# Values of a sliding-window attention kernel: staged per head with a ones column, moved 256 tokens at a time, read contiguously

## The chip, the cores and the metric

The kernel runs on one core of a Trainium2 chip. The core has a matrix engine (PE, whose weight loads are shown as a row of their own, PEld), three engines that work elementwise (DVE, ACT, POOL) and a sequencer, SP, that issues the DMA transfers; each of them takes its instructions in order and waits on semaphores. The metric is the device time of one execution in microseconds, as the median of the runs shown. Shorter is better.

## The reference

Two layers are run one after the other with the same weights; each is an attention block and a token mixer, both on normalised rows and both added to x. x has 2048 tokens of 512 values, 32 heads of 16 values, and a window of 256 tokens.

```python
def _A_ref(x, wqkv, wo):
    B, S, D = x.shape
    H = 32; Dh = D // H; W = 256
    qkv = (x @ wqkv).reshape(B, S, 3, H, Dh).transpose(2, 0, 3, 1, 4)
    q, k, v = qkv[0], qkv[1], qkv[2]
    scores = jnp.einsum("bhqd,bhkd->bhqk", q, k) * (Dh ** -0.5)
    idx = jnp.arange(S)
    mask = (idx[:, None] - idx[None, :] >= 0) & (idx[:, None] - idx[None, :] < W)
    scores = jnp.where(mask[None, None], scores, -1e9)
    p = softmax(scores, axis=-1)
    o = jnp.einsum("bhqk,bhkd->bhqd", p, v)
    return o.transpose(0, 2, 1, 3).reshape(B, S, D) @ wo

def _B_ref(x, w1, b1, w2, b2):
    h = layernorm(x)
    u = gelu(einsum("bsd,sf->bdf", h, w1) + b1)
    y = einsum("bdf,fs->bds", u, w2) + b2
    return y.transpose(0, 2, 1)

for _ in range(2):
    x = x + _A_ref(layernorm(x), A_wqkv, A_wo)
    x = x + _B_ref(layernorm(x), B_w1, B_b1, B_w2, B_b2)
```

## The kernel before

The program is a graph of operations. Each is created once, with the engine or engines that may run it, what it reads and what it writes. `ORDER`, a packed constant, holds the sequence of all 2487 operations and the engine chosen for each; `begin_order` unpacks it, `replay` hands out buffers in that sequence, and `emit` writes one instruction stream per engine and puts a wait wherever a result comes from another engine. So the order of the work is written out by hand beforehand, and nothing is decided on the chip. `cost`, `issue` and `prio` are figures for the search that made `ORDER`; in the program as it stands they do nothing.

**Attention.** Tokens are taken in four groups of 512 (`qkv`, m = 0 to 3). Normalised rows are transposed to xhT, on PE for the first group and by a DMA on SP (`tr`, L538) for the rest. PE makes keys (`fk`), queries (`fq`) and values (`fv`), all at L509 in steps of two 512-column matmuls (four of 256 columns in the split first group). DVE or ACT copies each result out of PSUM: L567 for queries, L589 for keys (staged in stg) and L619 or L621 for values (`evv`). The keys go on to kbd either by DVE or POOL (L603) or by eight small transfers on SP (`kz`, L598).

**Values.** `vproj` runs once for 128 tokens. Its copy goes to vst, ordered by half, by value index e and by group r of heads. Then `vz` (L624) issues four transfers on SP, one for each half of the tokens and each half h of the heads; each brings 64 partitions of 512 bytes to vb. In vb, [P, 3, 8, 17, 16], a block of 64 tokens has 17 rows of 16: 16 value indices and a row of ones, with the 16 heads of a half next to each other. The ones are written once per slot at the start, as three memsets on POOL (L457), and make the matmul produce the softmax denominators as a 17th output row. vb holds three groups of tokens, vst four blocks of 128 tokens.

**Scores and outputs.** For a chunk of queries, `sc` (L677) writes scores of 32 rows per head into two pairs of PSUM banks, four heads side by side on PE. ACT exponentiates each pair (`exp`, L692), POOL masks the blocks at the edge of the window (L713), and `pv` (L730) multiplies: eight matmuls of 64 rows by 17 columns side by side on PE, for two halves h and four heads r. The weights of each are 17 values of vb, `vb[64h:64h+64, slot, jj, :, 4o+r]`, so they lie 16 elements (32 bytes) apart. DVE transposes the result (L750), takes reciprocals (L754), POOL or DVE multiplies (`prod`, L756), and DVE transposes back (L761). `fwo` is the output projection, added to x at L772. Each of the two layers has 76 score groups, 152 exponentials of up to 1024 columns and 32 `pv` operations, which stand in the order mostly two by two.

**Mixer.** `fu` and `ful` (L509, L851) make u from w1 tiles that stream in (L786), ACT applies gelu (L866), and `fy` (L509) multiplies with w2 tiles (L798) and is added to x at L892. `fu`, `fwo`, `fy` and the projections are the fillers that `ORDER` puts between the score groups on PE. In the second layer the attention begins while the first layer's `fy` is still running.

The steps that the prediction follows are these: on SP the transfers `vz`, `kz`, `tr`, `w1` and `w2`; on DVE and ACT `evv`, `evk`, `evq` and `evka` (L577, L578); on POOL masks and `prod`; on PE `fv`, `sc` and `pv`. What replaces `vproj` and its two call sites is printed with the change; the old forms are here.

Of the kernel before, what the change touches and what calls it, by code (L numbers as in the profile page):

```python
# [15 lines left out]
    'c-qBRKd9<h8b8r<-^-mj1Bc}dWZ(?sK^8KQffOk+kbw-O$PN}Rq)6dHiY&NbVUdLt7VctU;erbm7P45lV38t)g@uI+78Vv378Vv37Pqjtg~csyv0uDiu'  # L16
    'ipFK%qy0iFL-l2f4}ed{l4GvqAn7}dL4-^Y&W9FK~WT%(O<(5BZQA1+h*2}9%D>xHJJLH3%1|yT{8@V?M~kOBzc~`vh^Qlvl(NfWV=f=N!1jhPNo~_8%'
    'a_WssH#W4F*zwwSw1dxtzru2BcA%jM7$n7`9rW)QIbm_I>t*j^q1Phnw8sl4O8ww`i*wimJ#TWJS^>#&!y2V?|N0i2G3#C4{P~s(c6M)M~YQJw%7$9T;'
    '0I7MsmxYgv}gIak)}8RyI8d{LcqKAjZ`+MaD6k)x`sc4xMq&24);ws*T-r_*Y+)*EngE`2kdPG<8Nv}Le#l`hi-;~rmg#wJrP!oEL7IR3g?jXF_P*I{M'
    '3R*uVY6vc5rj^j>;MbYEqV-!ctW|IY?h#QSYGf?WaI*DRJNU>N9!>|;FUZui<I<<eIw9KpAr*7fl;lZ_B*Ky{F<(F(q!9D19A6%ExKvjq8zHiy4F))l?'  # L20
    'j}e2!O+7YrqojtqPO0nO-<On9NvZCYvK_jF*mhDZCJA+=%q+?3bUK<M=|i0lhrOQE1AN6^uZ_D1OT68tmGPJ{DOs=A1kOe~zTG}NR@?2b3EAD>HwuM<<'
    '2c(ph+u+l?>C#t;jnSnR(q+Ysb$%#(Q36C3<kqNX5;ZVjz@#Zw9Ht)pQMTVPqW{5nBC&MQmND${XV4)Qmc2AZkNXrIM)UY<9Y)gal75t8=~kq)y)3vl*'
    '<laCyGiLO!>XC-z$o4h-*#L78+5f)2Xdn#2jf_qCl`8+MRBv+bhAQCD9N4dOh}a&+}lh=S7jOGstj>r@jK6oEg3@X^tz2reZKd*VZ##*A1PB!;z|~Oi?'
    'JkB_iasRs$|7)oO(hP6+e7uZl%ll3W)EOt;jK!c~Sf9dm`t8q|_Rj#kq&jHwEbNQmgVWmjTU;)Wq{HlH45obpk&lBQ{QfMDIN*v@Rzxm&Itmm6EmjElE'
    '@ur%%uMaH17fx4w8VK7t^8RsJ5(Cj%78+a+2L}ZnMt|)B18jnO0h|Pw~RiFwHkr<SMO08B3N@2MKW+}ieFc}B7<NBTsm6U<7-5Lhcb*Z^&$_z`0HwR-`'
    'NqM5-y432?CT-Nq%_gNxqERFvqL)e#Zk9F6(h$n<Qe4eZ6csqNn-@3k9~7u)HAxah8Oej)_hV)Bq1j5)4{{IuHdPe<qtz7uR{utdGq@|d?l>R@K@fz_p'
    '7S7tO83j(`cN>71@w~1q?euNLV_x8xstN*$eL=Q!r0d=1~@&B>Dbp+grI`#07#0i#RWn%hB3Bm3&}F#$VAA{F@8!JQ51x@O!}*Yh=a)lc4;$63FuE_RF'
    '6}=T21s=hXRixkr?H_xFJZAX()!A?cZn|8u(%VcSV*t(@aoOe1k{wXgURIkHD((b~hMox24jbN;8Zn;7B@c|BjYXNcspt5#0<r$mr^NuiNWFMiUS=U2i'
    '7{p<WO59v^$X9>zEAn8wXGXV>k!cw&R!X$nHwfr_a3-8ddJNwwZ1W=tAkBdV8S3{?X!t|3${7NMjILD&fjrJ}!4k@<tDNuuZ$5RxPtc;FbiZkfxau~@)'
    '{hFj1ycZAa|+zo?&Lm--Frx*}1jN;v$VKj|sy*4c<@5;2oOw$VfmGJ;RiV1bZ4hN`JK&fVIM?i+*P}Pw9GthN5pKDsAX=53UlF@iHh6BEJLQxX^VFEN9'  # L30
    'cGbb4+e_0F0tD~?1CaW|0VH_f`+a}qL$&vNf$u|_TCJ+WTv>*+SAY`8p^{Vdio0F0SdCUI%52*%*p}_#qFyiz2$IJn0`A)mu`G}Cz3r&qscW>>VK=0x8'
    'l^BQ-rwIRnVHss8Zg4Js@3atl>?i>GI`NNO<nqEPN)akg~mUlgO*y!j)GVavRD#?W^>3ij?;8HMX(v<BN_~$(S=laB7!I|)`K=~mo&}LV%K*I1wbRPOC'
    '`Tp%$634nNC^;AYkf-W@ITf<!Y5d^~)U4gb;v%@^rx*N4F1$2SD&{kC3`kRk$QKD^*>tmec=CM~0!Qi-j7^menPMK)XQj0U5MfUDWZ!VkUVrp6QEO76-'
    ';3gK|J<2!df9L{q;LJ>T;!&nSrE4~C&-ddEg^;SZBNMyy3?=debP=oZ%B2&M_zfU+MNlp@0J_mD|cm3fj>I7Sm%gQOOV01(i<AI81@pxrK4kl~eM&kHN'
    'Qk5L6xLf=8YZxOd(VpK#$uYg<^a)Y`$a$G7_kzA%Uq$`)vIj4*jn9Javi#1-W6$(-T#J7%W8;{Y0&X9M%T;3S~!G>UMxz{o-1F69^Jm$+3J2PjBCrN_w'
    'of&P(IIAvk*rhcHV;%%$9j9@-I)Kyx8)V!uZTN{(z@^ftZTi0B)Evilp&A@KhAaZ-bl3ARh8wh2vu)kBR4oWFmQ@)ND@p8Vz+5CD;0yX}d;iPB?=G6hw'
    'txfyq0c<vT{ah1yz~gdMKk+?k2?yd5kbfwKgZGRl|OcW`RwfbJo*A(o{-Pyvk3CpM%R{uM>xLUK{JPrpU<<Kr@6VO13ocHKxd!NG2Pr8qk4*1xSD(XhL'
    '10N>1);$zPQ>sf6hz(V~1W%6~Mnsj5A;I!fEcwMd5_HaDx2Y5OTR3yy0)|V)GZ6PW`9%#je69pnN{(BLf0@b_Su>r1(XH4Cm4R%5rZSuV^U<*IqyS{Q~'
    'bbpwA10%ele}p)aZadi!%ug^#oAV@L|<x3aHZ==iz$$Q_yWTuLW4<-R<RU8d#BS1X?@O1PrWt9+c^_yXZ0Mn_s_yIvL67x*bHPixLqi1DlPyUib2cMSA'
    'QzWiG$$ltyp*K3W*ouYn@Hg`SY2u|*bj5+i?Q#|4K+<zf6XYCNqq!Qp7K<_g_&0@qaf`c)BqmB4w8~pC{PyBVwJq3GaasIVD!3)1;LjG;(q89*j=nXu%'  # L40
    'Yp$GC_ZW5VN`y`lB>YMp<gd!=T!zA%y1OX4m%)$D{JgTuowF!hXulx5IDL6nT+b2C!tx>?$4f-GoQ__4pZkR8UVNIF`}}hLv;e=tSP)(feR7@ft4IES?'
    'd7g}xvquZSVe!;{tIrGU@i'
# [263 lines left out]
def bass_interleave_layers__sliding_block__mixer_token_mlp__prompt_kernel(  # L306
# [28 lines left out]
    with es:  # L335
# [9 lines left out]
        vb = sb("vb", [P, 3, 8, 17, 16])  # L345
        vst = sb("vst", [P, NVS, 512])
# [30 lines left out]
        p_w1, p_ul, p_vs = Pool("w1", 4), Pool("ul", 2), Pool("vs", NVS)  # L377
# [153 lines left out]
        def qkv(m, before, split, layer):  # L531
# [81 lines left out]
            def vproj(sp):  # L613
# [9 lines left out]
                def f_vz(e):  # L623
                    return [e.dma_start(vb[64 * h:64 * h + 64, tk.slot, 2 * sp + i, 0:16],  # L624
                                        vst[64 * i:64 * i + 64, ts.slot, 256 * h:256 * h + 256].rearrange("p (e r) -> p e r", e=16)) for i in range(2) for h in range(2)]
# [346 lines left out]
```

## Time and profile before

| What | us |
|---|---|
| median of 3 runs | 446.96 (446.56 to 448.96) |
| the profiled execution | 448.0 |
| its span in the profile | 446.3 |
| PE busy | 415.7 (93%) |
| ACT busy | 317.6 (71%) |
| DVE busy | 311.5 (70%) |
| POOL busy | 230.0 (52%) |
| transfers vb<-vst | 128 of 32 KB, 1.9 to land (median) |

The profiled execution took 448.0 us, of which 446.3 lie inside the span that the profile covers and 1.7 around it; it was 1.0 us above the median. Busy time of PE counts an instruction from its start to its modelled end, so a busy PE is not PE at its peak. Engine names in the profile are followed by the line of the kernel and by the tiles written and read, such as "PS<-pt,vb". "SPq" is SP's queue of transfers. The column after the bar is busy time and mean duration of one; after the second bar stands the idle time in front of these instructions and what ended it. The TensorE clock that was granted is 1.00 throughout, so no time depends on it here.

### The profile page before, as it was taken

What the parts mean: (1) busy time and instruction counts of PE and PEld (TensorE: products, weight loads), DVE (VectorE), ACT (ScalarE), POOL (GpSimd) and SP (SyncE); (2) the same over time, 40 slices, a digit from 0 to 9 for tenths busy, and PEclk for the clock granted to TensorE, in tenths of its full rate; (3) what the DMA queues carried; (4) which work ended last, traced back from release to release, by engine and by line L of the source; (5) the groups of instructions that cost most, each with busy time, mean ns of one, the idle gap of its engine ahead of it and who ended that gap; (6) DMA issues with size and microseconds to landing.
All of it is one profiled execution on the core that took longest, in us unless ns stands there. A gap on an engine that the chain in (4) does not pass through costs nothing.

```text
span 446.3 us, 13926 instructions
## 1 busy us (share of the span) xinstructions
PE 415.7 (93%) x5923; PEld 192.3 (43%) x5992; DVE 311.5 (70%) x570; ACT 317.6 (71%) x361; POOL 230.0 (52%) x351
## 2 busy tenths in 40 slices
PE   7888788989989999999999999999999999999997
PEld 6544333333433444444434444443444444444444
DVE  6998799878796569466557869988885767520323
ACT  4998999989999932518888999999999861440000
POOL 3496968797687631010649658768786551000000
PEclk9999999999999999999999999999999999999999
DMA  8634321302323357221454161212223274744443
GB/s 246 186 73 128 74 50 32 85 10 34 93 56 84 109 160 217 84 61 49 127 111 109 44 172 37 61 36 57 59 52 75 67 208 123 201 128 144 118 143 106
DMA packets 99758, 44.71 MB, mean 100 GB/s; under 512 B 29936, under 2 KB 99696, under 8 KB 99696
## 3 DMA queue, kind: packets, MB, share of 16 engines
q1 hardware_dynamic: 99696, 43.82, 37.4%
q8 instruction: 47, 0.77, 0.7%
q14 instruction: 15, 0.12, 0.1%
HBM read 33.56 MB, written 2.10 MB: 80 GB/s over the span
## 4 chain that ended last, share of the span: by engine, by line
PE 69%; ACT 15%; DVE 5%; SPq 4%; DMA 3%; issue 2%; POOL 1%
PE PS L509 46%; ACT pt L692 15%; PE PS L851 8%; PE PS L677 7%; PE PS L730 7%; SPq L598 2%; DMA xhT<-xh_sb 2%; PE PS L392 1%; DVE stats L467 1%; DMA w2b<-in_B_w_dram 1%; SPq L624 1%; POOL pt L713 1%; DMA w1b<-in_B_w_dram 1%; DVE x_sb L772 0%; DVE ul L756 0%
## 5 line engine op out<-in xcount | busy, mean ns | idle before, releaser
L692 ACT ACTIVATE pt<-PS 128x1024 bf16<-128x1024 f32 (+1 forms) x304 | 281.9, 1032 | 20.1 <-PE PS L677 17.4
L713 POOL TENSOR_TENSOR pt<-pt,ldm 128x256 int32<-128x256 int32 (+2 forms) x270 | 177.6, 683 | 72.2 <-ACT pt L692 68.2
L509 PE MATMUL PS<-uT,w2b 128*128 128x512 bf16 (+1 forms) x287 | 68.1, 369 | 1.3 <-DMA w2b<-in_B_w_dram 0.8
L509 PE MATMUL PS<-xhT,wqkv 128*128 128x512 bf16 (+1 forms) x270 | 63.7, 355 | 5.8 <-ACT pt L692 2.1
L509 PE MATMUL PS<-xh_sb,w1b 128*128 128x512 bf16 x265 | 65.8, 380 | 3.4 <-issue 1.9
L677 PE MATMUL PS<-qT,kbd 32*128 32x256 bf16 (+4 forms) x1488 | 60.4, 251 | 4.7 <-ACT pt L692 1.4
L892 DVE SCALAR_TENSOR_TENSOR x_sb<-PS,b2col,x_sb 128x512 bf16<-128x512 f32 x31 | 22.8, 746 | 50.1 <-PE PS L509 49.9
L480 POOL TENSOR_TENSOR rstd<-agg,mhalf 128x2 f32<-128x2 f32 (+1 forms) x33 | 22.6, 689 | 58.2 <-DVE agg L469 58.1
L750 DVE STREAM_TRANSPOSE rl<-PS 128x1024 f32<-128x1024 f32 x32 | 39.8, 1245 | 16.6 <-PE PS L730 16.2
L730 PE MATMUL PS<-pt,vb 64*17 64x320 bf16 (+4 forms) x2976 | 45.0, 259 | 5.0 <-ACT pt L692 1.7
L677 PEld LDWEIGHTS PS<-qT,kbd 32*128 32x128 bf16 x1488 | 21.7, 92 | 63.1 <-ACT pt L692 40.1
L866 ACT ACTIVATE uT<-rl,b1col 128x512 bf16<-128x512 f32 x28 | 18.6, 713 | 39.6 <-DVE rl L862 39.5
L467 DVE BATCH_NORM_STATS2 stats<-x_sb 128x6 f32<-128x512 bf16 x64 | 42.8, 679 | 2.2 <-DMA x_sb<-in_A_x_dram 1.7
L730 PEld LDWEIGHTS PS<-pt,vb 64*17 64x17 bf16 x2976 | 35.0, 110 | 18.4 <-POOL pt L713 6.7
L509 PE MATMUL PS<-uT,pt 128*128 128x512 bf16 x163 | 41.1, 379 | 0.5 <-issue 0.3
L509 PEld LDWEIGHTS PS<-uT,w2b 128*128 128x128 bf16 x294 | 27.3, 98 | 31.9 <-issue 2.7
L851 PE MATMUL PS<-xh_sb,w1b 128*128 128x512 bf16 x164 | 37.8, 379 | 0.3 <-issue 0.2
L509 PEld LDWEIGHTS PS<-xh_sb,w1b 128*128 128x128 bf16 x280 | 23.9, 97 | 33.0 <-issue 6.1
L509 PEld LDWEIGHTS PS<-xhT,wqkv 128*128 128x128 bf16 x288 | 24.0, 97 | 31.7 <-issue 5.6
L509 PE MATMUL PS<-wqkv,xhT 128*128 128x512 bf16 x117 | 33.1, 381 | 3.5 <-issue 1.4
L509 PE MATMUL PS<-wo_sb,oT 128*128 128x512 bf16 x119 | 30.7, 380 | 1.7 <-issue 1.0
L487 DVE TENSOR_SCALAR xh_sb<-x_sb,agg,rstd 128x512 bf16<-128x512 bf16 x64 | 29.1, 481 | 4.3 <-POOL rstd L480 4.2
(57 smaller groups left out, 318.5 us busy)
## 6 DMA issues: line engine op xcount, KB each, us to landing
w1b<-in_B_w_dram SPq DMA_DIRECT2D x112, 128.0 KB, 2.7
w2b<-in_B_w_dram SPq DMA_DIRECT2D x70, 128.0 KB, 2.6
pt<-in_B_w_dram SPq DMA_DIRECT2D x42, 128.0 KB, 2.8
vb<-vst SPq DMA_DIRECT2D x128, 32.0 KB, 1.9
out_dram<-x_sb SPq DMA_DIRECT2D x15, 128.0 KB, 1.8
x_sb<-in_A_x_dram SPq DMA_DIRECT2D x3, 512.0 KB, 8.3
wqkv<-in_A_wqkv_dram SPq DMA_DIRECT2D x4, 256.0 KB, 4.0
kbd<-stg SPq DMA_DIRECT2D x48, 16.0 KB, 2.0
```

Of the source, the lines that this page charges most:

```text
L467: op("vector:stat", lambda e: e.bn_stats(st[:, 0:6], x_sb[:, t, :]), reads=[f"x{t}"], writes=[("st", i)], cost=dve_cost(512))
L480: op("gpsimd:rstd", lambda e: e.tensor_tensor(rstd[:, t0:t1, 0], agg[:, t0:t1, 1], mhalf[:, 0:1].to_broadcast([P, t1 - t0]), op=ALU.pow), ...
L487: op("vector:xh", lambda e: e.tensor_scalar(xh_sb[:, t, :], x_sb[:, t, :], agg[:, t, 0:1], rstd[:, t, :], op0=ALU.subtract, op1=ALU.mult), ...
L509: return e.matmul(o, lhsT=w, rhs=x, start=start, stop=stop, skip_group_check=True)
L677: last = e.matmul(bank(tt[r // 2], r % 2)[:, base + c0 * 64:base + (c0 + n) * 64], lhsT=kbd[32 * r:32 * r + 32, tk.slot, o, jj].rearrange( ...
L692: op("scalar:exp", lambda e, ts=ts, tp=tp, i=i, cols=cols: e.activation(probs(tp)[:, i, 0:cols, :], pair(ts)[:, :, 0:cols].rearrange("p r ...
L713: return e.tensor_tensor(v, v, m, op=ALU.mult)
L730: last = e.matmul(bank(t, h)[32 * r:32 * r + 17, i + q0 * 64:i + (q0 + n) * 64], lhsT=vb[64 * h:64 * h + 64, tk.slot, jj, :, 4 * o + r], r ...
L750: op("vector:od", lambda e, t=tod, tr=tr: e.transpose(rl[:, tr.slot:tr.slot + 2].rearrange("p a b -> p (a b)"), pair(t)), reads=[(tod, i) ...
L851: last = e.matmul(bank(tu, tt), lhsT=v()[:, sc - b0, k0 + tt * P:k0 + (tt + 1) * P], rhs=xh_sb[:, sc, :], start=(sc == b0), stop=(sc == NT ...
L866: op("scalar:gelu", lambda e, ft=ft, tt=tt: e.activation(uT[:, ft, :], rl[:, tmps[tt].slot], ACTF.Gelu_apprx_tanh, bias=b1col[:, ft:ft + 1 ...
L892: op("vector:resy", lambda e: e.scalar_tensor_tensor(x_sb[:, t, :], bank(ft), b2col[:, t:t + 1], x_sb[:, t, :], op0=ALU.add, op1=ALU.add), ...
```

## The change

The values are staged and moved in another layout, and the order is another.

- vb becomes [P, 3, 8, 16, 17]: for each head of a half 16 values and a one, next to each other. `pv` reads its 17 weights as one run of 34 bytes.
- vst becomes [P, 4, 2, 16, 17] and holds the ones itself: one memset writes them in all four slots at the start, and the three memsets of vb go. The copies (`evv`) write runs of 16 values 17 apart and wait for this memset. `pv` no longer waits for the ones.
- `vproj` now makes two blocks of 128 tokens, with two neighbouring slots of vst and two copies, and `vz` issues four transfers for the 256 tokens. Each brings 64 partitions of two runs of 544 bytes. 64 transfers do what 128 did.
- `ORDER` is replaced. It holds 2469 operations: two memsets and 16 `vz` fewer.

Unpacked with `begin_order`, and with each operation called by its name in the graph, the two orders compare as follows (before, after):

| Engine | operations | what differs in kind |
|---|---|---|
| PE | 922, 922 | nothing |
| ACT | 357, 360 | evk 0, 4; evq 4, 6; evt 5, 4; evv 4, 3; evu 4, 3 |
| DVE | 553, 554 | prod 15, 20; evk 24, 20; evq 32, 30; kz 9, 8; evt 3, 4; evu 38, 39; evv 28, 29 |
| POOL | 338, 331 | prod 17, 12; memsets of ones 3, 1 |
| SP | 317, 302 | vz 32, 16; kz 6, 7 |

On PE the 152 score groups stand in the same sequence. The work that stands ahead of each of them, counted with the same duration for an operation of the same kind, differs by at most 2.6 us, and from the 128th score group on by nothing.

```diff
@@ tiles
-        vb = sb("vb", [P, 3, 8, 17, 16])
-        vst = sb("vst", [P, NVS, 512])
+        vb = sb("vb", [P, 3, 8, 16, 17])
+        vst = sb("vst", [P, NVS, 2, 16, 17])
...
-        p_w1, p_ul, p_vs = Pool("w1", 4), Pool("ul", 2), Pool("vs", NVS)
+        p_w1, p_ul, p_vs = Pool("w1", 4), Pool("ul", 2), Pool("vs", NVS, True)
@@ ones
-        ONES = [("one", i) for i in range(3)]
-        two_ones = 1.0 + 0x3F80 / 2.0 ** 23
-        for i in range(3):
-            f_one = lambda e, i=i: e.memset(vb[:, i, :, 16].bitcast(dt.float32), two_ones)
-            op("gpsimd:one", f_one, reads=["mhalf"], writes=[("one", i)], cost=150, alts=[("vector", f_one, 150)])
+        f_one = lambda e: e.memset(vst[:, :, :, :, 16:17], 1.0)
+        op("gpsimd:one", f_one, reads=["mhalf"], writes=["one"], cost=200, alts=[("vector", f_one, 200)])
@@ qkv
-            def vproj(sp):
-                ft, ts = filler(m == 0), Tile(p_vs)
-                mm_group("fv", ft, 4, lambda c: (bank(ft), xhT[:, tx.slot, c, sp * P:(sp + 1) * P], wqkv[:, c, 1024:1536]),
-                         [(tx, sp)] + [("w2", o) for o in range(4)], holds=[tk, ts])
-                src = lambda: bank(ft).rearrange("p (r h e) -> p h e r", h=2, e=16)
-                dst = lambda: vst[:, ts.slot].rearrange("p (h e r) -> p h e r", h=2, e=16)
...
+            def vproj(sp0):
+                ts = Tile(p_vs, 2)
+                for k in range(2):
+                    sp, ft = sp0 + k, filler(m == 0)
+                    mm_group("fv", ft, 4, lambda c, sp=sp, ft=ft: (
+                        bank(ft), xhT[:, tx.slot, c, sp * P:(sp + 1) * P], wqkv[:, c, 1024:1536]),
+                        [(tx, sp)] + [("w2", o) for o in range(4)], holds=[tk, ts])
+                    src = lambda ft=ft: bank(ft).rearrange("p (r h e) -> p h r e", h=2, e=16)
+                    dst = lambda k=k: vst[:, ts.slots[k], :, :, 0:16]
+                    op("vector:evv", lambda e, src=src, dst=dst: e.tensor_copy(dst(), src()), reads=[ft, "one"], writes=[(ts, k)],
+                       cost=dve_cost(512, psum=True), prio=-2e5,
+                       alts=[("scalar", lambda e, src=src, dst=dst: e.copy(dst(), src()), act_cost(512))])
...
                 def f_vz(e):
-                    return [e.dma_start(vb[64 * h:64 * h + 64, tk.slot, 2 * sp + i, 0:16],
-                                        vst[64 * i:64 * i + 64, ts.slot, 256 * h:256 * h + 256].rearrange("p (e r) -> p e r", e=16)) for i in range(2) for h in range(2)]
-                op("sync:vz", f_vz, reads=[ts], writes=[(tk, "v", 2 * sp + i) for i in range(2)], cost=2500, dma=True, parts=4,
-                   issue=2000.0, prio=-2e5)
+                    return [e.dma_start(
+                        vb[64 * h:64 * h + 64, tk.slot, 2 * sp0 + i:2 * sp0 + i + 3:2].rearrange("p s r e -> p s (r e)"),
+                        vst[64 * i:64 * i + 64, ts.slot:ts.slot + 2, h].rearrange("p s r e -> p s (r e)"))
+                        for i in range(2) for h in range(2)]
+                op("sync:vz", f_vz, reads=[(ts, k) for k in range(2)], writes=[(tk, "v", 2 * sp0 + i) for i in range(4)], cost=2500,
+                   dma=True, parts=4, issue=2000.0, prio=-2e5)
...
-                for sp in vs[:2]:
-                    vproj(sp)
+                vproj(vs[0])
...
-                for sp in vs[2:]:
-                    vproj(sp)
+                if vs[2:]:
+                    vproj(vs[2])
@@ attention, f_pv
-                                            lhsT=vb[64 * h:64 * h + 64, tk.slot, jj, :, 4 * o + r],
+                                            lhsT=vb[64 * h:64 * h + 64, tk.slot, jj, 4 * o + r, :],
...
-                        rd = list(ONES)
+                        rd = []
```

More of the change, by code (lines that the diff above doesn't have):

```diff
@@ L20 @@
[L20 to L39, printed above, removed]
```

37 lines of the change are left out of this document (27 added, 10 removed).

## The prediction

> **What bounds the kernel now.** I read the page first, then the busy times by stretches of 20 us, then the waits, and last the rows of single instructions around the values.
>
> ```profile
> PE 415.7 (93%) x5923; PEld 192.3 (43%) x5992; DVE 311.5 (70%) x570; ACT 317.6 (71%) x361; POOL 230.0 (52%) x351
> ...
> PE   7888788989989999999999999999999999999997
> ```
> ```profile
> 20.00:40.00 20.00, 16.76 (x438) 9.40 (x434) 17.64 (x36) 18.31 (x21) 16.40 (x24) 1.00 0.43 109
> ...
> 60.00:80.00 20.00, 18.02 (x343) 7.65 (x344) 19.22 (x40) 19.96 (x23) 15.46 (x23) 1.00 0.11 24
> ...
> 120.00:140.00 20.00, 18.08 (x374) 8.08 (x383) 16.58 (x33) 19.68 (x22) 16.56 (x26) 1.00 0.17 43
> ...
> 280.00:300.00 20.00, 19.40 (x344) 8.67 (x348) 17.29 (x33) 18.41 (x20) 13.79 (x21) 1.00 0.25 53
> ...
> 400.00:420.00 20.00, 19.95 (x93) 9.08 (x93) 3.00 (x4) 0.00 (x0) 0.00 (x0) 1.00 0.40 118
> ```
>
> The columns of the second view are PE, PEld, DVE, ACT and POOL. PE idles 446.3 - 415.7 = 30.6 us in all, most of it before 140 us. In the first layer's attention (20 to 160 us) ACT is the tightest engine, 19.96 of 20 us in one stretch; in the second layer's (220 to 360) PE is, at 19.4 of 20; after 365 us PE alone works. So an instruction more on ACT costs time in the first layer, a wait of PE costs it in the second, and nothing on SP or POOL costs any unless something late comes of it. What can be won at all lies in the waits:
>
> ```profile
> POOL pt L713 <- ACT pt L692: 68.2, 61, 11.8
> ...
> PEld PS L730 <- POOL pt L713: 6.7, 13, 1.8
> ...
> PE PS L730 <- DMA vb<-vst: 1.6, 1, 1.6
> ...
> PEld PS L509 <- DMA w1b<-in_B_w_dram: 0.8, 1, 0.8
> ```
>
> Values were late once, by 1.6 us; w1 once, by 0.8. The rows of what is edited:
>
> ```profile
> L730 PEld LDWEIGHTS PS<-pt,vb 64*17 64x17 bf16 x2976 | 35.0, 110 | 18.4 <-POOL pt L713 6.7 <-issue 5.8 <-ACT pt L692 4.1
> ...
> L677 PEld LDWEIGHTS PS<-qT,kbd 32*128 32x128 bf16 x1488 | 21.7, 92 | 63.1 <-ACT pt L692 40.1 <-issue 10.9 <-DVE qT L567 2.9
> ```
> ```profile
> 48.63 5.01 SPq L624 DMA_DIRECT2D vb<-vst  x8
> ...
> 56.18 0.44 PEld L730 LDWEIGHTS PS<-pt,vb 64*17 64x17 bf16 x40 [1.84 <-POOL pt L713]
> 56.21 0.69 PE L730 MATMUL PS<-pt,vb 64*17 64x64 bf16 x40 [1.64 <-DMA vb<-vst]
> ...
> 97.55 6.16 SPq L598 DMA_DIRECT2D kbd<-stg  x8
> ```
>
> The first pair shows that 17 weights 32 bytes apart take 110 ns to load where 128 adjacent ones take 92. The second shows the one late transfer: eight issues in a row on SP, and a `pv` that the masks of POOL held until the same moment.
>
> **The change part by part**, against the profiled execution (448.0 us: 446.3 of span and 1.7 around it, 1.0 above the median); the sum is then taken off the median.
>
> *Weights read side by side.* In the records of single matmuls, the next matmul on the same part of PE starts 55 ns after one of 64 columns in `pv` and 39 ns after one of 64 columns in `sc`; at 128 columns both take 66. So the load shows only behind the 68 groups of 64 columns: 68 x 16 ns = 1.1 us. At the head of each of the 64 `pv` operations the difference of the two loads, 18 ns, may show as well: 1.2 us. Half of all this lies in the first layer, under ACT. I take -1.0. Bounds: 0, and 372 groups of eight x 18 ns = -6.7 if every load were exposed; a loss is not excluded by any row with runs of 34 bytes, so +1 on that side (the same 64 operations by 18 ns).
> The row gives 110 against 92 ns. The Trainium skill ("SBUF — State Buffer", section "Door 1: The DMA port swizzle (why `[64,N]` ≈ `[32,N]`)", note on cachelines) says that reads crossing to a new 16-byte line at every element pay a penalty, which would make the new load shorter, as the two rows suggest; by it the term stays at -1.0. Against the change speaks "TensorE: Matmul & The Clock Gate", section "LDWEIGHTS (loading the stationary operand)", of the Trainium skill, where a load depends on its number of columns alone: by that the term is 0 and the sum below -1.7. The rows do not bear it out, since 17 columns take longer here than 128.
>
> *Copies and memset.* The copies take 680 ns (DVE, x28) and 594 ns (ACT, x4); plain copies of the same size to stg take 682 ns with contiguous operands, so the pattern costs nothing now, and I take 0 for the new one. Ends: 32 copies by +-10%, +-2. Three memsets of 150 ns go from POOL and one of about 200 comes (a memset of ident takes 204); it must only precede the first copy at 12.4 us, and POOL waited 3.6 us at 14 us. 0; without that cover 0.2.
>
> *Transfers.* 64 issues fewer at 0.6 us are 38 us of SP's time, and one `kz` more (eight issues) takes 5 back. This counts only where SP was behind. That was from 97.55 to 121 us, where issues follow each other without a gap and PE then waits 0.8 us for w1; and at 56.2 us, where the wait of 1.6 was covered by POOL's until 56.18, so that its worth is between 0 and 1.6, nearer 0: I take 0.5. Together -1.3; ends 0 and -7 (all the stalls of PE and PEld on DMAs: xhT 3.4, w2b 1.7, vb 1.6, w1b 0.8, rounded down).
>
> *Waiting for 256 tokens.* The first block's values now wait for the second block's copy. After that copy the way to `pv` is 0.69 us of copying, four issues (2.4) and the landing (1.9): 5.0 us. Behind each transfer on SP the next `tr`, `w1` or `kz` waits too. The cover is the PE work between the last value matmul of a pair and the first `pv` that reads it. For the first pair it is, by the new order, four score groups x 0.40, two transposes x 0.30 and eight fillers x 0.44 (two 512-column matmuls) = 5.7 us. The five shortest covers come to 5.6, 5.7, 6.0, 6.1 and 6.8 us, against 5.0, 5.3, 6.0, 6.0 and 7.3 for the shortest before. All exceed 5.0, so I take 0; with the cover gone each costs what its copy is late, and PE's scores behind that `pv` wait with it.
>
> *Work between engines.* ACT gets three operations more, in the first layer 0.4 us on balance (two query copies 0.39, one transpose copy 0.59 and one key copy 0.60 come, two key copies of 0.48 and one copy of 0.60 go), and 1.4 in the second, where ACT has 1 to 2 us of slack in 20. POOL loses five products of 1.06 us; `pv` waited 6.7 us for POOL's masks, and I credit 0.3 of it, as the masks mostly wait for ACT themselves (68.2 us). DVE gets these products (0.93 each) and loses others, net +1.7, of which I charge 0.3 in stretches where it is busy 17 to 19 us of 20. Together +0.4; ends -5 and +4.
>
> *Order.* The work ahead of each score group differs by at most 2.6 us and by nothing from the 128th on. Score groups 9 to 21 (about 15 to 45 us) stand 0.4 to 1.3 us earlier; ACT idles 1.7 us from 20 to 40 and 1.3 from 40 to 60, and I take -0.8. Groups 25 to 37 stand 0.4 to 1.8 later, in the stretch where ACT is full and has scores waiting: 0, or +1.8 if none wait.
>
> Sum: -1.0 - 1.3 + 0 + 0.4 - 0.8 = -2.7. From 446.96 that is 444.3 us.
>
> **Rivals.** *Slower: values late in the first layer.* The covers exceed the way by 0.6 to 1.1 us at three places before 60 us and one near 110, DVE is busy 88 to 96% of the stretches from 20 to 80 us, and a copy stands behind at least one other instruction of 0.4 to 1.3 us. From about 1 us of queueing PE stops in front of `pv`, the next scores stand behind it, and ACT, the tight engine, runs dry. 1.5 us at each of the four places, 6.0, less the gain of 2.7: +3.3, 450.3 us. For it: the wait of 1.6 at 56.2 us came at such a place. Against it: there POOL held the same `pv`.
> *No difference.* The work on PE is the same 922 operations and ACT's is 152 exponentials per layer; SP's lost time lies beside it. Then the stalls move by a few tenths each and it ends near 446.5. For it: only 2.4 us of waits name the values or w1. This holds too if the weights load no faster and nothing else goes wrong: 445.3.
> *Much faster.* Every load exposed, -6.7, with the rest: about 439. Against it: the 66 ns for 128 columns on both sides.
>
> **How the numbers follow.** This kernel's runs lie within 0.5% of each other but for one, so I take 0.5% (2.2 us) as what can be told. My forecast has 0.37, much faster 0.06, no difference 0.25, late values and other new waits of the order 0.32. Most of the first two lies beyond 2.2 us: faster 0.42; slower 0.31; the rest, 0.27, within. The range leaves a tenth on each side: 438.5, a little past the much faster case, to 452.0, a little past the late values. The likeliest case's own range is 442 to 446.
>
> **What would show it.** Right: loads of L730 at or below 92 ns; 64 issues of vb<-vst of 68 KB and about 0.6 us each; no wait of `pv` on vb<-vst above 0.5 us; ACT's first exponential at the same 9.5 us, and the last one of the first layer 1 to 2 us earlier; PE idle 28 us. Wrong: waits of L730 on vb<-vst or on the copies before 60 us, with ACT idle above 3 us between 20 and 60; or longer copies at L619. A stage that grows without any value being late would mean that the new order itself, which I compared only by work ahead of the scores, decides.

## The result, and the profile after

The changed kernel took 442.38 us (median of 4 runs, 441.43 to 443.99) beside 447.35 us of the kernel before on the same chip (446.56 to 448.96): a ratio of 0.9888, with an interval of 0.9846 to 0.993. So it is 5.0 us faster, where 2.7 was forecast. The difference is real, and its size is what needs explaining. Three later comparisons on other chips gave 5.8, 6.5 and 5.6 us. A part of these three is the granted clock of TensorE. In the 51 later runs of the kernel before its mean over the run was 0.999 or more in 10 (mean time 447.9 us), about 0.996 in 33 (448.7) and 0.992 in 8 (450.2); in the 15 later runs of the changed kernel it was 0.999 or more. By the runs at 0.999 or more alone, which for the kernel before are two, one and four, the three differences are 5.4, 5.9 and 5.1 us. The profiled execution took 441.94 us with a span of 440.2; before, these were 448.0 and 446.3.

The page of the changed kernel, the lines of busy time and of PE's slices:

```profile
PE 422.9 (96%) x5992; PEld 187.6 (43%) x5992; DVE 311.1 (71%) x570; ACT 318.5 (72%) x364; POOL 225.4 (51%) x344
...
PE   7998998999999999999999999999999999999996
```

PE has 5992 matmuls here as it has weight loads, while the page of before had 5923: 69 records were missing there. What they are worth is seen where the changed kernel was profiled again: with 5992 matmuls PE was busy for 422.9 and 422.6 us, in a trace with 5923 for 413.3. So, if the same matmuls are missing there, before's PE worked some 9.5 us more than its page says, and idled about 21 us and not the 30.6 from which the prediction starts. Against that, 17.3 us idle here is a small step. Neither page alone shows where the time went. The stretches of the changed kernel, with the same columns as before (length, then PE, PEld, DVE, ACT, POOL, granted clock, DMA share, GB/s):

```profile
20.00:40.00 20.00, 17.68 (x443) 8.41 (x442) 19.29 (x42) 19.89 (x23) 15.94 (x23) 1.00 0.45 90
...
60.00:80.00 20.00, 17.58 (x406) 7.48 (x409) 16.24 (x31) 19.95 (x23) 17.43 (x27) 1.00 0.30 59
...
120.00:140.00 20.00, 18.78 (x348) 7.65 (x346) 16.52 (x32) 19.86 (x22) 15.65 (x24) 1.00 0.33 72
...
280.00:300.00 20.00, 19.99 (x394) 8.61 (x379) 18.05 (x33) 19.18 (x22) 15.41 (x24) 1.00 0.34 77
...
400.00:420.00 20.00, 20.00 (x100) 9.49 (x98) 5.79 (x8) 0.00 (x0) 0.00 (x0) 1.00 0.44 132
```

ACT is full from 20 us on, where before it had 18.31 of 20: it still bounds the first layer, and it no longer runs dry between 20 and 40 us. PE is full in the second layer (19.99 of 20). The waits of the changed kernel (total, times, longest):

```profile
POOL pt L715 <- ACT pt L694: 78.4, 67, 9.4
...
PEld PS L506 <- DMA w2b<-in_B_w_dram: 2.9, 4, 1.0
...
PEld PS L732 <- POOL pt L715: 5.6, 14, 0.5
```

No wait of PE on vb, xhT or w1b is left. The one on w2b has grown, from 1.7 us to 2.9. The groups by shape:

```profile
L732 PEld LDWEIGHTS PS<-pt,vb 64*17 64x17 bf16 x2976 | 31.3, 85 | 17.2 <-POOL pt L715 5.6 <-issue 5.4 <-ACT pt L694 3.1
...
L679 PEld LDWEIGHTS PS<-qT,kbd 32*128 32x128 bf16 x1488 | 21.7, 93 | 65.1 <-ACT pt L694 44.8 <-issue 7.5 <-DVE rl L752 2.8
...
L454 POOL MEMSET vst<- 128x128 bf16 x1 | 0.7, 650 | 0.0
```

The load of the 17 weights fell from 110 to 85 ns, while that of `sc` (L679) is as it was. The memset of the ones takes 650 ns, three times the estimate.

A better measure than sums is when the exponentials start, since the two kernels run the same 304 in the same sequence. The exponentials are counted from 0, and the figures are starts in the changed kernel less those before:

| exponential | before at, us | change, us |
|---|---|---|
| 0 | 9.5 | -0.3 |
| 24 | 32.1 | -1.2 |
| 32 | 41.0 | -2.6 |
| 56 | 64.9 | -2.2 |
| 88 | 96.4 | -4.2 |
| 151, last of the first layer | 157.7 | -4.7 |
| 152, first of the second | 207.3 | -6.9 |
| 160 | 215.1 | -4.4 |
| 168 | 225.5 | -6.5 |
| 303, last | 362.2 | -8.1 |
| end of span | 446.3 | -6.1 |

The gain comes in steps at a few places, and 2.0 us of it are given back after the last exponential. The step at the 152nd is not kept: at the 160th it is gone. A single trace also scatters: in three more traces of the changed kernel the 32nd exponential starts 0.6, 1.0 and 1.1 us later than in this one, and the last 0.3, 0.8 and 1.2 us later. So a step of 1 us between two single traces can be chance, above all at the start.

### The profile page after: what moved, and what is told of

It reads as the page before. It is cut to its first block, busy times and chain, and to the rows that moved or that the text cites. A ratio compares the mean times of both kernels' runs of the same rounds, so it can differ in the third digit from the quotient of the medians.

```text
span 440.2 us, 13923 instructions
## 1 busy us (share of the span) xinstructions
PE 422.9 (96%) x5992; PEld 187.6 (43%) x5992; DVE 311.1 (71%) x570; ACT 318.5 (72%) x364; POOL 225.4 (51%) x344
## 4 chain that ended last, share of the span: by engine, by line
PE 71%; ACT 19%; DVE 3%; POOL 3%; DMA 2%; issue 1%; SPq 0%; DVEq 0%
PE PS L506 49%; ACT pt L694 19%; PE PS L853 8%; PE PS L679 7%; PE PS L732 7%; POOL pt L715 3%; DMA w2b<-in_B_w_dram 2%; DVE stats L464 1%; DVE rl L752 1%; DMA x_sb<-in_A_x_dram 0%; DVE xh_sb L484 0%; DVE x_sb L774 0%; PE PS L542 0%; DVE vst L620 0%; DVE x_sb L894 0%
## 5 line engine op out<-in xcount | busy, mean ns | idle before, releaser
L715 POOL TENSOR_TENSOR pt<-pt,ldm 128x256 int32<-128x256 int32 (+1 forms) x270 | 177.2, 682 | 78.9 <-ACT pt L694 78.4
L506 PE MATMUL PS<-uT,w2b 128*128 128x512 bf16 (+1 forms) x294 | 69.7, 370 | 1.1 <-DMA w2b<-in_B_w_dram 0.9
L506 PE MATMUL PS<-xhT,wqkv 128*128 128x512 bf16 (+1 forms) x288 | 67.1, 358 | 2.7 <-ACT pt L694 0.8
L506 PE MATMUL PS<-xh_sb,w1b 128*128 128x512 bf16 x280 | 69.0, 381 | 0.4 <-ACT pt L694 0.3
L679 PE MATMUL PS<-qT,kbd 32*128 32x256 bf16 (+4 forms) x1488 | 60.7, 252 | 5.5 <-ACT pt L694 3.7
L679 PEld LDWEIGHTS PS<-qT,kbd 32*128 32x128 bf16 x1488 | 21.7, 93 | 65.1 <-ACT pt L694 44.8
L868 ACT ACTIVATE uT<-rl,b1col 128x512 bf16<-128x512 f32 x28 | 18.7, 714 | 39.9 <-DVE rl L864 39.9
L732 PE MATMUL PS<-pt,vb 64*17 64x320 bf16 (+4 forms) x2976 | 43.0, 252 | 2.1 <-DVE x_sb L774 0.6
L732 PEld LDWEIGHTS PS<-pt,vb 64*17 64x17 bf16 x2976 | 31.3, 85 | 17.2 <-POOL pt L715 5.6
L506 PEld LDWEIGHTS PS<-xh_sb,w1b 128*128 128x128 bf16 x280 | 23.9, 98 | 32.1 <-issue 5.7
L853 PE MATMUL PS<-xh_sb,w1b 128*128 128x512 bf16 x168 | 37.0, 380 | 0.0
L484 DVE TENSOR_SCALAR xh_sb<-x_sb,agg,rstd 128x512 bf16<-128x512 bf16 x64 | 30.6, 498 | 7.6 <-POOL rstd L477 7.6
L506 PE MATMUL PS<-wqkv,xhT 128*128 128x512 bf16 x128 | 34.4, 381 | 0.2 <-ACT pt L694 0.2
L506 PE MATMUL PS<-wo_sb,oT 128*128 128x512 bf16 x128 | 32.5, 381 | 0.3 <-DVE oT L763 0.2
```

The costliest lines, as they stand in the source:

```text
L484: op("vector:xh", lambda e: e.tensor_scalar(xh_sb[:, t, :], x_sb[:, t, :], agg[:, t, 0:1], rstd[:, t, :], op0=ALU.subtract, op1=ALU.mult), ...
L506: return e.matmul(o, lhsT=w, rhs=x, start=start, stop=stop, skip_group_check=True)
L679: last = e.matmul(bank(tt[r // 2], r % 2)[:, base + c0 * 64:base + (c0 + n) * 64], lhsT=kbd[32 * r:32 * r + 32, tk.slot, o, jj].rearrange( ...
L715: return e.tensor_tensor(v, v, m, op=ALU.mult)
L732: last = e.matmul(bank(t, h)[32 * r:32 * r + 17, i + q0 * 64:i + (q0 + n) * 64], lhsT=vb[64 * h:64 * h + 64, tk.slot, jj, 4 * o + r, :], r ...
L853: last = e.matmul(bank(tu, tt), lhsT=v()[:, sc - b0, k0 + tt * P:k0 + (tt + 1) * P], rhs=xh_sb[:, sc, :], start=(sc == b0), stop=(sc == NT ...
```

## The experiments

The theory with which I began is that of the forecast: three parts that add up, each small. Its rivals are that one part alone brings the gain, and that the new order is only what makes the long transfers bearable. The first four kernels take the three parts one by one.

**New order and long transfers, weights strided as before.**

```diff
-        vb = sb("vb", [P, 3, 8, 16, 17])
-        vst = sb("vst", [P, NVS, 2, 16, 17])
+        vb = sb("vb", [P, 3, 8, 17, 16])
+        vst = sb("vst", [P, NVS, 2, 17, 16])
...
-                                            lhsT=vb[64 * h:64 * h + 64, tk.slot, jj, 4 * o + r, :],
+                                            lhsT=vb[64 * h:64 * h + 64, tk.slot, jj, :, 4 * o + r],
```

> The changed kernel with the weights 32 bytes apart again: vst and vb keep the value index outside the heads, the ones are a 17th row of vst and travel with the 544-byte runs; the 256-token transfers and the new order stay. Theory weights (the adjacent read shortens every group of eight matmuls in pv: 22 ns at 64 columns x 68 groups and about 6 ns at the other 304, 3.3 us in all): 3 us slower than the changed kernel, about 445.5, loads of pv back at 110 ns. Theory order (the new sequence brings most of the gain): within 1 us of the changed kernel, 442 to 443.5. Theory transfers (SP freed of 64 issues): the same, 442 to 443.5.

Measured: 443.67 us (443.2 to 444.38) beside 448.28, ratio 0.9897 (0.9866 to 0.9929). Loads are back at 110 ns, the memset, now of contiguous elements, at 205.

**Long transfers and adjacent weights in the old order.** The only edit is `ORDER`, which is the old sequence again; each pair's one `vz` stands where the later of the two stood, and one of them had to be moved ahead, past an `exp` and a mask, so that it precedes the `pv` that reads it.

> The changed kernel with the order of before: each transfer of 256 tokens stands where the later one of its two transfers of 128 stood (one of the sixteen is three places earlier, ahead of a pv that reads it), everything else where it was. Theory weights: keeps most of the gain, 443.5 to 444.5. Theory transfers: also keeps a gain, 444 to 446, with SP free by 97 to 121 us. Theory order: the gain is gone, 446.5 to 448.

Measured: 444.79 us (442.2 to 445.83), ratio 0.9918 (0.9887 to 0.9948). The median is no better than that of the next run, all of whose executions lie within the spread of these, so adjacent weights show no gain here. The trace shows what stands against one. Early on POOL:

```profile
4.47 0.65 POOL L453 MEMSET vst<- 128x128 bf16 x1
4.73 0.95 POOL L476 TENSOR_TENSOR rstd<-agg,mhalf 128x1 f32<-128x1 f32 x1
```

In the old order the strided memset stands ahead of the second rstd (L476; with a contiguous memset of 0.20 that one takes 0.56), and the first exponential is 0.5 us later than in the next run. By the 48th it is 1.8, of which 0.8 come behind a late `pv` at 54 us, after which the granted clock falls (last section); from there to the last one 1.3 us are won back, a little at every `pv`.

**Long transfers alone**: old order as in the last, weights strided as in the first.

> Old order as in the run before, weights 32 bytes apart, transfers of 256 tokens: the transfers alone. Theory transfers: 1.5 to 3 us faster than the kernel before (444.5 to 446). Theories weights and order: no gain, 447 to 448, or 1 us slower where the first 128 tokens now wait for the second copy.

Measured: 444.54 us (443.98 to 444.89), ratio 0.9914 (0.9885 to 0.9942): 3.7 us under the kernel before.

**Adjacent weights alone**, in the kernel before, with 128-token transfers of one run of 544 bytes:

```diff
-        vb = sb("vb", [P, 3, 8, 17, 16])
-        vst = sb("vst", [P, NVS, 512])
+        vb = sb("vb", [P, 3, 8, 16, 17])
+        vst = sb("vst", [P, NVS, 2, 16, 17])
...
-                    return [e.dma_start(vb[64 * h:64 * h + 64, tk.slot, 2 * sp + i, 0:16],
-                                        vst[64 * i:64 * i + 64, ts.slot, 256 * h:256 * h + 256].rearrange("p (e r) -> p e r", e=16)) for i in range(2) for h in range(2)]
+                    return [e.dma_start(vb[64 * h:64 * h + 64, tk.slot, 2 * sp + i].rearrange("p r e -> p (r e)"),
+                                        vst[64 * i:64 * i + 64, ts.slot, h].rearrange("p r e -> p (r e)")) for i in range(2) for h in range(2)]
...
```

> The kernel before with its order, its 128-token transfers (now one run of 544 bytes per partition) and the adjacent weights; the three memsets write the ones of vst. Theory weights: 3 us faster than before, about 444.5, loads of pv at 85 ns. Theories order and transfers: within 1 us of before, 446.5 to 448.

Measured: 447.7 us (445.42 to 449.43, 12 runs), ratio 0.9976 (0.9951 to 1.0001). A gain of 0.6 us that can't be told from none. In its trace the exponentials start 0.5 us ahead of the kernel before, lose 1.8 at one place (at 11 us PE waits 2.0 us instead of 1.3, and then the clock falls), lose 1.3 more at 58 us, where a `pv` waits 2.6 us for values and the clock falls again, are 2.4 behind at the 56th and 0.5 ahead again at the last: 2.9 us won on the way.

What follows from the four: the transfers alone bring 3.7 of the 5 to 6 us (3.2 by the three and four runs at a clock of 0.999 or more). The order then adds 0.9 (444.54 less 443.67), though the spreads of the two runs overlap. The split depends on the sequence in which the parts are added: with adjacent weights in place the order brings about 2 us (from a ratio of 0.9918 here to 0.9872 on another chip), and the weights bring nothing measurable before the order is there. The traces show how the transfers do it. The kernel before, its timeline (start, duration, engine, instruction, and in brackets the idle time before it and what ended it):

```profile
26.02 5.80 SPq L624 DMA_DIRECT2D vb<-vst  x8
...
33.34 1.39 PEld L730 LDWEIGHTS PS<-pt,vb 64*17 64x17 bf16 x128 [1.46 <-ACT pt L692]
33.37 1.63 PE L730 MATMUL PS<-pt,vb 64*17 64x64 bf16 x128 [1.29 <-ACT pt L692]
...
35.39 2.85 ACT L692 ACTIVATE pt<-PS 128x1024 bf16<-128x1024 f32 x3 [1.33 <-PE PS L677]
```

The same place with long transfers alone:

```profile
25.57 2.56 SPq L624 DMA_DIRECT2D vb<-vst  x4
...
31.81 1.35 PEld L731 LDWEIGHTS PS<-pt,vb 64*17 64x17 bf16 x128 [0.29 <-ACT pt L693]
31.81 1.62 PE L731 MATMUL PS<-pt,vb 64*17 64x64 bf16 x128
```

Before, eight issues in a row end at 31.82. The last of them starts at 31.22, so that with the landing of 1.9 its values are there at about 33.1; `pv` starts at 33.34. The profile puts this wait down to ACT, whose exponentials run on without a break. But with long transfers `pv` starts 0.04 us after an exponential ends at 31.77, and before, the same exponential ended at 32.13, more than 1 us ahead of `pv`. With four issues the wait is gone, and so are the 1.33 us in which ACT runs dry behind it: the exponentials of this kernel are 0.4 us early up to the 24th and 1.7 at the 32nd. Another step is like it. At 218 us before:

```profile
215.32 2.41 SPq L624 DMA_DIRECT2D vb<-vst  x4
217.84 1.26 SPq L538 DMA_TRANSPOSE xhT<-xh_sb  x1
...
220.34 0.55 PEld L509 LDWEIGHTS PS<-wqkv,xhT 128*128 128x128 bf16 x4 [0.53 <-DMA xhT<-xh_sb]
```

The same place with long transfers alone:

```profile
207.73 2.55 SPq L624 DMA_DIRECT2D vb<-vst  x4
211.54 1.28 SPq L534 DMA_TRANSPOSE xhT<-xh_sb  x1
```

Before, issues follow each other on SP from 204.20 to 219.10 us with hardly a gap, sixteen of them values transfers, and the transpose goes out at 217.84. With long transfers SP runs empty ahead of it and it goes out at 211.54, 6.3 us earlier in a kernel that is 2.8 us ahead there. The waits on xhT and w2b at 220 to 225 us are gone, and the lead grows to 4.0. The wait on w1b at 117 us goes in the same way (to 3.0): with long transfers no values transfers stand right ahead of those loads.

A third step is not of this kind. At 90 us before:

```profile
85.80 1.27 SPq L538 DMA_TRANSPOSE xhT<-xh_sb  x1
...
90.48 1.04 PE L509 MATMUL PS<-xhT,wqkv 128*128 128x512 bf16 x3 [1.10 <-DMA xhT<-xh_sb]
```

The transpose stands on SP behind four values transfers (82.23 to 85.75). With long transfers it stands behind four of them too (80.93 to 84.24) and goes out at 84.28, 1.5 us earlier, of which 1.2 are the lead that the kernel has by then. But it lands 2.5 us after its issue, and before it took 4.6. So its wait is gone, and the lead grows from 1.2 us at the 80th exponential to 2.3 at the 88th. Why the landing was slower is not shown; with weights alone it took 4.3 us at this place, in the old order with long transfers and adjacent weights 2.5.

The kernel loses something too, at 53 us:

```profile
46.23 5.15 SPq L624 DMA_DIRECT2D vb<-vst  x8
...
53.11 0.92 PE L731 MATMUL PS<-pt,vb 64*17 64x64 bf16 x56 [1.71 <-POOL pt L714]
...
54.41 7.44 ACT L693 ACTIVATE pt<-PS 128x1024 bf16<-128x1024 f32 x8 [1.72 <-PE PS L678]
```

Here the values of two pairs come late, and 1.0 us of the lead is lost: the rival of late values, in the old order. The profile names a mask, but the last of the eight issues starts at 50.77 and lands at 52.86. At 90 us and at 253 us further waits of `pv` are put down to vb by name (0.5 and 0.9 us), and by the 200th exponential 0.7 us more of the lead are gone. In the changed kernel the same eight issues stand at 44.31 (5.48 us), the next `pv` at 52.50 waits 0.42 us and for masks, and no `pv` waits on vb anywhere. That is part of what the order brings.

**The changed kernel, and with strided weights, side by side on another chip.**

> The changed kernel itself once more, on the chip of the two runs beside it, so that they can be compared without the detour over the kernel before. Every theory: 0.985 to 0.993 of the kernel before, about 442.5.

> The changed kernel with the weights 32 bytes apart again, beside the changed kernel on one chip. By the traces the adjacent weights bring 2.3 us up to the last exponential and 1.7 at the end: 1.5 to 2 us slower than the changed kernel. If they bring nothing: within 0.5 us of it.

Measured: 442.47 us (441.62 to 443.3), ratio 0.9872 (0.9848 to 0.9896), and 443.7 (443.47 to 444.37), ratio 0.9902 (0.988 to 0.9924), beside 448.23. In the new order adjacent weights are worth 1.2 us, and the two spreads do not touch. The traces of this pair show where. At the 32nd exponential the changed kernel is 0.2 us behind its strided form, at the 151st it is level with it, at the last it leads by 1.0, and at the end by 1.1. So the gain is made in the second layer. Between the 32nd and the 144th ACT is the bound, and little is gained there. The first traces of the two kernels, from different chips, differ more: 1.0 us by the 24th exponential already, 2.3 at the last, 1.7 at the end. The early 1.0 can't be put down to the weights: it comes with a wait of 0.7 us for a transposed tile at 26 us, and the second trace of the changed kernel has such a wait too (0.5). From the 151st to the last exponential the first pair gives 0.9 us and the second 1.0.

**Eight transfers of 128 tokens at the same place**, behind the second copy:

```diff
-                        vb[64 * h:64 * h + 64, tk.slot, 2 * sp0 + i:2 * sp0 + i + 3:2].rearrange("p s r e -> p s (r e)"),
-                        vst[64 * i:64 * i + 64, ts.slot:ts.slot + 2, h].rearrange("p s r e -> p s (r e)"))
-                        for i in range(2) for h in range(2)]
+                        vb[64 * h:64 * h + 64, tk.slot, 2 * sp0 + i + 2 * k].rearrange("p r e -> p (r e)"),
+                        vst[64 * i:64 * i + 64, ts.slots[k], h].rearrange("p r e -> p (r e)"))
+                        for k in range(2) for i in range(2) for h in range(2)]
...
```

> The changed kernel with its 256 tokens moved by eight transfers of 128 tokens instead of four: same place in the order, same layout, 64 issues more on SP (38 us of its time at 0.6). Theory issues (what was late before stood behind issues on SP): 2 to 3 us slower than the changed kernel, 444.5 to 445.5, with waits on xhT, w1b or vb back. Theory place (the gain comes from where the transfers stand, and from the adjacent weights): within 1 us, 442 to 443.5.

Measured: 471.59 us (469.98 to 475.55), ratio 1.0533 (1.0495 to 1.057): 29 us above the changed kernel. Its chain of waits, by engine:

```profile
PE 63%; ACT 14%; SPq 9%; DMA 6%; DVE 3%; POOL 3%; issue 1%; DVEq 0%
```

SP's queue, which holds less than half a per cent of the changed kernel's chain, holds 9% of this one. In the profiled execution, the slowest of the six (475.55 us), the exponentials fall behind in jumps: 5.1 us by the 32nd, 9.6 by the 48th, 18.7 by the 88th, 33.4 at the last. `pv` waits 10.4 us on vb, five times. So behind the second copy there is room for four issues and not for eight. Not all of the loss is waiting: the mean granted clock of this trace is 0.967, and 3.3% of 473.8 us is 16 us, an upper estimate of what the lowered clock takes.

**The early halves first.** To part the place from the number of issues, each block has its own four transfers, by the code of the run with adjacent weights alone, and `ORDER` is the changed one with two `vz` for one: the first block's right behind its own `evv`, the second block's where the changed order has its `vz`. The ones are written by three memsets instead of one.

> The changed kernel's order and weights, but each 128-token block has four transfers of its own (34 KB each), and those of the first block of a pair are issued right behind its own copy, as before; only the second block's four stand where the changed kernel has its four. So the path behind the second copy is as short as in the changed kernel, and what is added is SP time alone: 64 issues more, 64 x 0.64 = 41 us of SP over the run. Theory (the transfers' gain of 3.7 us is SP's queue time, paid at a few single waits where a vb, xhT or w1b issue stands late on SP): 445 to 448, that is 2.5 to 5.5 above the changed kernel, waits on xhT, w1b or vb by name are back, and the run of eight issues that cost 29 us is not repeated. Rival (the changed kernel's gain lies in how the transfers land, 68 KB against 34, or in the copies that need no hurry, not in SP's queue): 442 to 443, at most 0.5 above the changed kernel.

> The changed kernel on the same chip, to set the run with the early halves against: 442.4, 0.987 to 0.990 of the kernel before.

Measured: 471.44 us (469.7 to 473.96), ratio 1.0482 (1.0449 to 1.0515), beside 443.23 (441.75 to 444.0), ratio 0.9843 (0.9818 to 0.9867), for the changed kernel. Both figures that I gave were far off: 28 us lost, not 2.5 to 5.5 and not none. The exponentials fall behind at four places: 6.5 us by the 24th, 6.1 more by the 120th, 7.9 between the 184th and 192nd, 9.6 between the 224th and 232nd. The third, in the timeline of this kernel:

```profile
251.48 0.69 DVE L617 CAST vst<-PS 128x512 bf16<-128x512 f32 x1 [1.37 <-PE PS L507]
252.20 3.10 SPq L622 DMA_DIRECT2D vb<-vst  x4
255.35 2.12 SPq L796 DMA_DIRECT2D w2b<-in_B_w_dram  x4
...
258.29 1.04 PE L507 MATMUL PS<-uT,w2b 128*128 128x512 bf16 x2 [5.12 <-DMA w2b<-in_B_w_dram]
```

And the same four loads of w2b in the changed kernel:

```profile
228.62 2.01 SPq L800 DMA_DIRECT2D w2b<-in_B_w_dram  x4
```

There they go out 10 us ahead of the values (238.95). With the early halves SP had nothing to do from 249.63 on: a values transfer stood at its head and waited for a copy, the loads stood behind it, and PE then waited 5.1 us for them. At the fourth place it waits 7.9 us: SP stands idle from 284.56 to 294.13 behind a values transfer, and then sixteen issues (11.1 us) go ahead of the load. At the start a load of x that the changed kernel issues at 9.49 goes out at 17.81. Most of what is left of the third jump, 7.9 us in all, is the clock. Three stretches of 4 us (length, PE, PEld, DVE, ACT, POOL, granted clock, DMA share, GB/s):

```profile
254.00:258.00 4.00, 0.00 (x0) 0.00 (x0) 1.82 (x4) 0.34 (x1) 0.00 (x0) 0.91 0.36 102
258.00:262.00 4.00, 3.71 (x20) 1.11 (x20) 0.00 (x0) 1.94 (x2) 0.06 (x1) 0.50 0.47 129
262.00:266.00 4.00, 4.00 (x96) 1.65 (x98) 2.38 (x4) 1.35 (x2) 1.36 (x2) 0.73 0.48 124
```

After the wait PE ran at 0.50 and then 0.73, which by an estimate from these figures is worth 4 x 0.50 + 4 x 0.27 = 3.1 us. Over the whole trace the mean clock is 0.977, and 2.3% of 470 us is 11 us: at most so much of the loss is lowered clock, which comes behind the waits. So this kernel pays first for transfers that could have gone and were held up behind one that could not, then for the clock; the issuing itself counts at the fourth place. That leaves open how much of the 3.7 us is the time of 64 issues and how much is what stands behind them; it shows that on SP a place in the sequence can cost more than all the issues together.

**The old tail.** After the last exponential the changed kernel loses 2.0 us of its lead. Its timeline there:

```profile
380.18 7.67 SPq L800 DMA_DIRECT2D w2b<-in_B_w_dram  x8
...
388.81 0.55 PEld L506 LDWEIGHTS PS<-uT,w2b 128*128 128x128 bf16 x4 [1.01 <-DMA w2b<-in_B_w_dram]
...
393.02 1.41 PEld L506 LDWEIGHTS PS<-uT,w2b 128*128 128x128 bf16 x8 [0.64 <-DMA w2b<-in_B_w_dram]
...
395.34 1.41 PEld L506 LDWEIGHTS PS<-uT,w2b 128*128 128x128 bf16 x8 [0.92 <-DMA w2b<-in_B_w_dram]
```

The new order begins the output matmuls (`fy`) with tiles of w2 that are still on their way. In the next kernel, whose only edit is in `ORDER`, all operations after the 138th score group stand in the old order's sequence, which begins them with tiles of pt that came earlier and mixes them with the last steps of `ful`. Everything before that is the changed kernel.

> The changed kernel whose operations after the 138th of 152 score groups stand in the sequence of the kernel before: there the first output matmuls of the second layer start with the w2 tiles in pt, between the last u matmuls, and w2b had landed when it was wanted. If the 2 us that the changed kernel loses again after the last exponential (its lead over before falls from 8.1 to 6.1 us) are its waits for w2b, this gains 1 to 2 us on the changed kernel, about 441. If that lead is lost to something that the second half of the old order shares, no change.

Measured: 440.82 us (440.47 to 442.9), ratio 0.9845 (0.9819 to 0.9872), 1.65 under the changed kernel on the same chip. As the spreads overlap, the two were compared once more:

> The changed kernel with the old tail once more, beside the changed kernel on the same chip, since the two spreads of the first comparison overlap (440.47 to 442.9 against 441.62 to 443.3). If the waits for w2b in the last stage are the cause of what the new order loses there, it is again 1 to 2 us under the changed kernel; if the first comparison was chance, within 0.5 us.

> The changed kernel on the same chip, to set the old tail against: 442 to 443, 0.985 to 0.990 of the kernel before.

Measured: 440.77 us (440.68 to 441.53), ratio 0.9834 (0.9807 to 0.986), beside 442.43 (441.19 to 443.31), ratio 0.9866 (0.9839 to 0.9893): 1.66 again, with an overlap of 0.3 us. In the trace of the first of the two the same tiles are read without a wait, for instance:

```profile
392.33 3.33 PEld L505 LDWEIGHTS PS<-uT,w2b 128*128 128x128 bf16 x16
```

No wait on w2b is left in either trace. In the first of them the exponentials from the 24th on are 0.2 to 0.5 us later than in the first trace of the changed kernel, and the end is 1.1 earlier; beside the changed kernel of the same chip the last exponential is 0.7 earlier in the one pair and 0.4 later in the other, and the stretch behind it 1.8 and 1.6 us shorter. So 1.65 us of the new order's worth are lost in its tail, and this kernel is faster than both.

## Why the prediction was right, and where it was wrong

The direction, the range and the likeliest case's own range (442 to 446) held; the size came out at nearly twice the forecast. Step by step:

- **Weights, -1.0: right in sum, not in its working.** Measured -1.2 in the new order, and nothing that can be told from none in the old one. In single records the next matmul on the same part of PE starts 33 ns after one of 64 columns instead of 55 (22 ns, not 16), and the wider ones gained as well: 66 to 60, 93 to 87, 117 to 114, 146 to 142 ns. With the groups of each width (68, 64, 68, 60 and 112) that is 2.9 us of PE work, the same that the kernel with the weights alone won back on its way. PE's busy time shows 1.8 of it (424.7 us with strided weights and 422.9 with adjacent ones, on one chip, where neither trace lacks a record). The first layer absorbs what lies under ACT, as the prediction had it: this pair is level at the 151st exponential and 1.1 us apart at the end of the span. The bound of 0 by "columns alone" falls: 17 columns took 110 and 85 ns, and only their distance differs. By the Trainium skill's page "SBUF — State Buffer" (section "Door 1: The DMA port swizzle (why `[64,N]` ≈ `[32,N]`)", note on cachelines), elements that each open a new 16-byte line are read more slowly than neighbours; both rows agree with it.
- **Copies and memset, 0: right.** Copies take 688 and 605 ns (680 and 594 before). The memset took 650 ns, not 200. In the changed order it stands between two masks at 12.89 us, and in the first traces of the two kernels no exponential is more than 0.1 us later than with the memset of 205. In the old order, ahead of the second rstd, it cost 0.5: "without that cover 0.2" was too little.
- **Transfers, -1.3: the term that was mis-sized.** Measured -3.7, two thirds of the whole gain. "This counts only where SP was behind" was right; the list of two places was not. I looked for waits that name vb or w1. One of 1.3 us, at 33.37, is named ACT. Those on xhT (3.4 us in all) and w2b (1.7) stood in the very view that I read, and I kept them for the end of the range instead of asking what stood ahead of these transfers on SP. About 1.1 us of the gain came at 90 us with a transpose that landed 2 us sooner, for a reason that is not shown. At 56.2 us, for which 0.5 was credited, the old order in fact lost 1.0 with long transfers. The reading of that place was not right either: the mask ahead of this `pv` ends at 55.70 and the values land at 56.08, so the masks did not hold it until 56.18.
- **Waiting for 256 tokens, 0: right for the changed kernel, by little.** No `pv` waits on vb. In the old order it does, 1.7 us at 53.11, 0.5 at 90 and 0.9 at 253 us, and with four issues more behind the copy 10.4 us in all: the cover of 5.6 to 6.8 us holds 5.0 and not 7.6 (four more issues by 0.64).
- **Order, -0.8: right in sum by two errors.** Measured -0.9 with strided weights, in spreads that overlap, which is a gain of about 2.5 up to the tail (0.9 and the 1.65 that the old tail brings back) and the 1.65 lost there. With adjacent weights it is about -2. "From the 128th on by nothing" compared the work ahead of score groups only; which w2 tiles the last stage reads, and when SP issues them, was not looked at.
- **Work between engines, +0.4:** not tried by itself, and not shown. It came with the new order, so it is contained in that step. The steps of -3.7, -0.9 and -1.2 lead from the one kernel to the other, so their sum of -5.8 is near any measured difference whatever this term is worth.
- **Rivals.** Late values are real, and the new order is what keeps them out. No difference failed with its argument that "only 2.4 us of waits name the values or w1". Every load exposed did not come: 2.9 of 6.7.
- **Signs.** Loads at 85 ns, 64 transfers of 68 KB, no wait on vb, ACT's first exponential: as said. The last exponential of the first layer came 4.7 us earlier, not 1 to 2, which marked the term above. PE's idle time could not be compared, as 69 matmuls were missing from the trace of before.

## What to carry to other kernels

A queue that issues in order is read by what stands behind each of its entries, not by the waits that name the data it carries: look at every late transfer of any kind and ask what was issued just ahead of it and how long it took to land, and distrust a wait on an engine that was busy without a break. Fewer, longer transfers pay where such a queue is the hidden link; adding issues, or putting one that waits for a copy ahead of loads that could go, cost 29 and 28 us here, partly by the lowered clock that followed the waits. Compare two kernels by pairs of traces from one chip, and know how far two traces of one kernel lie apart before a step between two kernels is believed. When an order is replaced as a whole, compare its last stage too, including which buffers it reads first.

## What the runs showed of the hardware

**The granted clock can fall after a short gap.** In the old order with long transfers and adjacent weights, two stretches of 4 us, with the columns of the stretches above:

```profile
50.00:54.00 4.00, 2.26 (x17) 0.72 (x15) 2.90 (x6) 3.72 (x5) 4.00 (x6) 1.00 0.51 111
54.00:58.00 4.00, 3.53 (x116) 1.59 (x116) 2.05 (x3) 1.82 (x2) 1.89 (x3) 0.57 0.77 134
```

PE was busy for 2.26 of 4 us, with one gap of 1.76 us in front of `pv`, and in the next 4 us the clock was 0.57. With weights alone it is the stretch from 10 to 20 us:

```profile
10.00:20.00 10.00, 7.72 (x86) 4.22 (x88) 7.46 (x23) 7.59 (x12) 2.98 (x7) 0.83 0.73 221
```

There a wait of PE of 2.0 us came first; before, PE waited 1.3 us at this place and the clock stayed at 1.00. With long transfers alone a gap of 1.7 us at 53 us left it at 1.00. In finer stretches the clock was 0.50 for 3.4 us, from 54.3 to 57.7 and from 11.9 to 15.3; in the 3.4 us ahead of these PE was busy for 1.48 and 1.43 us, and with long transfers alone, where it did not fall, for 1.54 (49.7 to 53.1). No limit follows from this: with the early halves 0.92 us of work in the 3.4 us from 19.6 on left the clock at 1.00. So a gap of about 2 us can cost more than itself, but does not always. One such stretch of 3.4 us at half lowers the mean of a run of 447 us by 0.4%, so the means of 0.996 and 0.992 of the kernel before fit one and two of them. The Trainium skill ("TensorE: Matmul & The Clock Gate", section "HAM oscillation — how this bites in real kernels") puts the limit for idle gaps of PE at about 3.4 us; here gaps of 1.8 and 2.0 came before a lower clock, while with the early halves it fell during longer ones, of 5.1 and 7.9.

**A strided memset is slow on POOL.** 128 elements of 2 bytes a partition took 650 ns at a distance of 34 bytes and 205 in runs of 16 side by side, while the copies into rows of 17 took hardly longer than before (688 against 680).

**A trace can lack matmuls without a sign.** About half of the traces here show 5923 of 5992, always 69 too few, and with them some 9.5 us of PE's busy time; the same kernel shows both.
